# Attention and gated MLP on one core: the low-word step of the float64 weight conversion moved from VectorE to GpSimd

## The chip, the core and the metric

One core of a Trainium2 chip. The metric is the device time of one execution in microseconds; the kernel before takes 406.13 us (median of 3 runs, 405.83 to 406.23). The engines are TensorE (PE in the profile; its weight loads are PEld), VectorE (DVE), ScalarE (ACT), GpSimd (POOL) and SyncE (SP), whose queue issues all transfers of this kernel.

## What is computed

For each of 8 batches and 8 heads, 32 packed queries `p` attend over 576 keys and values, and the 576 queries `q` then attend over the 32 packed results. The heads are put side by side (512 features) and go through a gated layer. Cut to what matters:

```python
p_packed = sm_attn(p, k, v)                  # softmax(p k^T / 8) v
x = sm_attn(q, p_packed, p_packed)           # heads side by side: (8, 576, 512)
h = np.maximum(x @ w_in, 0.0)                # w_in 512 x 1024
conv_out = sum of conv_w[t] * h shifted by t - 1 along the sequence, t = 0, 1, 2
out = (h * sigmoid(conv_out)) @ w_out        # w_out 1024 x 512
```

`q`, `k`, `v` and `p` are float32. `w_in`, `conv_w` and `w_out` are float64, and the kernel has to make float32 of them on the chip.

## The kernel before

The work is cut into 16 groups (a batch and four of its heads), g = 0 to 15. `attention(g)` does both attentions of a group; `packed_weight(b, hf)` multiplies the packed results of a batch into `w_in` (line 609, L609); `ffn1(b, j)` makes one 128-feature block of the hidden layer (matmuls L661; then Relu L673 and scaling L677 on ScalarE, two multiply-adds L679 and L683 on VectorE, Tanh L687 on ScalarE, product L689 on VectorE); `ffn2(m)` multiplies 128 rows by `w_out` (L752, after a split into high and low parts L700 and L703).

The order of all instructions is written out in a table, `ORDER`, of 1525 stream numbers. Each stream is a generator that yields a `Step` (engine, cost in ns, events and buffers it needs) just before it issues its instructions. `Flow.run` takes the streams in the table's order, and every engine executes its own instructions in that order. `Flow` also keeps a planned time for each step, from the costs and from the lags in `LAG` (from engine to engine) and `ISSUE` (for engines whose steps are transfers). That plan has one effect on the program: until the first `ffn2` matmuls, `Flow.fill` puts idle matmuls (`warm`, L244, 216 ns each in the plan) where the plan sees TensorE waiting.

The weights come in eight pieces of 1 MB, i = 0 to 7 (0 to 3 are `w_in`, 4 to 7 `w_out`); L295 issues their transfers in the order 2, 0, 1, 5, 3, 4, 6, 7. They land in three slots, `stage` for i = 2 and 5 and two parts of `spare` (the second `hgt` buffer) for the others; the transfer of piece i waits until piece i - 3 has been converted (`("wp", i - 3)`). `conv_w` has a transfer of its own. Each piece then goes through `narrow`, on 128 partitions with 1024 float64 numbers each, seen as pairs of 32-bit words:

- L265, ScalarE: the upper words, rescaled in place (sets `("up", key)`);
- L267, VectorE: the top three bits of each low word, in place (every second word, so a step of 8 bytes);
- L272, VectorE: upper word shifted left by three, or-ed with those bits, written to `w_in_sb` (i under 4) or to `tmp`.

A piece of `w_out` is then split into `wo_hi` (L323) and `wo_lo` (matmuls L328, copy L332). The L267 step is `loose`: it needs the landed data alone, not the ScalarE step before it in its stream. In the ORDER table it has a place among VectorE's other steps. In the attention, L559, L583 and L417 are transposes on VectorE, L495, L563 and L572 reductions (all of one tensor operand), L565, L578 and L589 have two tensor operands, as L272, L679, L683, L689 and L703 have. L589 makes the low part `a2lo` of the second attention's weights, which L661 needs beside the high part; L629 is the ScalarE copy that makes `glo`, the low part of the folded weight.

Of the kernel before, what the change touches and what calls it, by code (L numbers as in the profile page):

```python
# [63 lines left out]
class Flow:  # L64
# [12 lines left out]
        "PE": dict(PE=0, ACT=197, DVE=196, SP=200, POOL=200),  # L77
        "ACT": dict(PE=216, ACT=153, DVE=142, SP=200, POOL=200),
        "DVE": dict(PE=256, ACT=128, DVE=127, SP=200, POOL=200),
        "DATA": dict(PE=300, ACT=300, DVE=300, SP=0, POOL=0),  # L80
    }
    ISSUE = dict(SP=(465, 1100), POOL=(1050, 1000))
    LATER, LANES = 620, 8
    SLOW = ((4600, 1.28), (5500, 1.7))

# [57 lines left out]
    def transfers(self, step, at):  # L143
        issue, delay = self.ISSUE[step.engine]
        for _ in range(step.parts):
            if step.engine == "SP":
                at = max(at, self.flights.pop(0))
            at += self.LATER if step.engine == "SP" and self.issued >= self.LANES else issue
            self.issued += step.engine == "SP"
            slow = next((x for t, x in self.SLOW if self.data < t), 1.0)  # L150
            self.data = max(self.data, at + delay) + step.ns / step.parts * slow
            if step.engine == "SP":
                self.flights.append(self.data)
        return at, self.data

    def run(self, order):
        for n in order:
# [6 lines left out]
            if engine == "PE":  # L164
# [4 lines left out]
                self.tiled = step.tiled  # L169
            elif step.engine in self.ISSUE:  # L170
                self.free[engine], t = self.transfers(step, at)
# [13 lines left out]
def tile_packed_attention_conv_gate(  # L185
# [11 lines left out]
    nc = tc.nc  # L197
# [61 lines left out]
    def narrow(key, out, raw, m, after=(), take=(), sets=None):  # L259

        pair = raw.rearrange("r (c t) -> r c t", t=2)
        up = pair[:, :, 1]
        low = pair[:, :, 0]
        yield Step("ACT", 93 + m * 14 // 15, after=after, sets=[("up", key)])
        nc.scalar.activation(out=up, in_=up, func=AF.Prelu, scale=F64_REBIAS, alpha=-(2.0**32))  # L265
        yield Step("DVE", 68 + m * 100 // 192, after=after, loose=True)
        nc.vector.tensor_scalar(  # L267
            out=low.bitcast(I32), in0=low.bitcast(U32), scalar1=2.0**-29, scalar2=7.0, op0=ALU.mult, op1=ALU.min
        )
        yield Step("DVE", 69 + m * 100 // 96, after=[("up", key)], take=take, sets=sets)  # L270
        out = out()
        nc.vector.scalar_tensor_tensor(  # L272
            out=out,
            in0=up.bitcast(I32),
            scalar=3,
            in1=low.bitcast(I32),
            op0=ALU.logical_shift_left,
            op1=ALU.bitwise_or,
        )
# [17 lines left out]
    def weight(i):  # L297
# [3 lines left out]
        if i < 4:  # L301
            dst = w_in_sb[:, c : c + 2, cols]
            if src.dtype != F32:
                yield from narrow(i, lambda: dst.bitcast(I32), st, DFF, after, sets=[("wp", i), ("w", i)])
            else:
                yield Step("DVE", 1135, after=after, sets=[("wp", i), ("w", i)])
                nc.vector.tensor_copy(out=dst, in_=st.rearrange("r (c f) -> r c f", c=2))
            return
# [7 lines left out]
        if src.dtype != F32:  # L316
            yield from narrow(i, whole, st, DFF, after, ["x"], [("wp", i)])
        else:
            yield Step("DVE", 1135, after=after, take=["x"], sets=[("wp", i)])
            whole()  # L320
            nc.vector.tensor_copy(out=wide[0], in_=st)
# [12 lines left out]
    def conv_weight():  # L334
        src = conv_w.rearrange("k (j c) -> (k j) c", c=128)
        yield Step("SP", 60, take=["s2"], sets=["cd"])
        st = wk.tile([128, S], F32, name="s2", tag="s2")
        if conv_w.dtype != F32:
            nc.sync.dma_start(out=st[: 3 * NJ, :256].bitcast(I32), in_=src.bitcast(I32))
            yield from narrow("conv", lambda: cw_raw.bitcast(I32), st[: 3 * NJ, :256], 128, ["cd"])  # L340
        else:
            nc.sync.dma_start(out=cw_raw, in_=src)
        yield Step("PE", 20, take=["sm"], give=["s2"], cols=20)
        t = small()
        nc.tensor.transpose(out=t[:, : 3 * NJ], in_=cw_raw, identity=ident[: 3 * NJ, : 3 * NJ])
        yield Step("ACT", 71, give=["sm"], sets=["cw"])
        nc.scalar.copy(out=cw, in_=t[:, : 3 * NJ])
# [473 lines left out]
```

## Time and profile before

| | before |
|---|---|
| median of 3 runs | 406.13 us (405.83 to 406.23) |
| profiled execution: first to last instruction (span) | 404.4 us |
| TensorE busy | 395.5 us, 98% |
| VectorE busy | 340.2 us, 84% |
| ScalarE busy | 275.2 us, 68% |
| GpSimd busy | 0.9 us, 12 instructions |
| chain that ended last | PE 74%, DMA 8%, ACT 8%, DVE 5%, SP queue 3% |
| granted TensorE clock | 1.000 of full speed |

The runs' times include what lies before the first and after the last instruction; the profile has the span alone, so the profiled execution's own time stands only as those 404.4 us, 1.7 us under the median of the runs. Busy time is the union of the instructions of an engine. Matmuls are pipelined, so that a busy TensorE may be running or holding a matmul back; what it waits for is read from the list of waits and from the chain that ended last, which goes back from the last instruction to whatever released each step.

### The profile page before, as it was taken

What the parts mean: (1) busy time and instruction counts of PE and PEld (TensorE: products, weight loads), DVE (VectorE), ACT (ScalarE), POOL (GpSimd) and SP (SyncE); (2) the same over time, 40 slices, a digit from 0 to 9 for tenths busy, and PEclk for the clock granted to TensorE, in tenths of its full rate; (3) what the DMA queues carried; (4) which work ended last, traced back from release to release, by engine and by line L of the source; (5) the groups of instructions that cost most, each with busy time, mean ns of one, the idle gap of its engine ahead of it and who ended that gap; (6) DMA issues with size and microseconds to landing.
All of it is one profiled execution on the core that took longest, in us unless ns stands there. A gap on an engine that the chain in (4) does not pass through costs nothing.

```text
span 404.4 us, 8231 instructions
## 1 busy us (share of the span) xinstructions
PE 395.5 (98%) x3319; PEld 317.6 (79%) x3319; DVE 340.2 (84%) x494; ACT 275.2 (68%) x475; POOL 0.9 (0%) x12
## 2 busy tenths in 40 slices
PE   7899999999999999999999999999999999999996
PEld 6668677787868878888778788788687878887886
DVE  0789999999999999999999999999889886557220
ACT  4889999977668486867566756687666676655121
POOL 0000000000000000000000000000000000000000
PEclk9999999999999999999999999999999999999999
DMA  8999999997947876496563715316001000010211
GB/s 298 366 366 233 293 257 163 137 157 128 134 96 105 129 190 128 88 186 103 107 99 99 151 55 101 129 30 113 28 2 52 28 18 35 26 53 0 78 53 52
DMA packets 140377, 49.19 MB, mean 122 GB/s; under 512 B 121244, under 2 KB 132788, under 8 KB 140340
## 3 DMA queue, kind: packets, MB, share of 16 engines
q1 hardware_dynamic: 140340, 48.67, 53.9%
q8 instruction: 26, 0.43, 0.5%
q14 instruction: 11, 0.09, 0.1%
HBM read 37.25 MB, written 9.44 MB: 115 GB/s over the span
## 4 chain that ended last, share of the span: by engine, by line
PE 74%; DMA 8%; ACT 8%; DVE 5%; SPq 3%; issue 1%; ACTq 0%
PE fo L752 42%; PE big L661 19%; PE sm L752 3%; DMA hgt<-in_moe_w_in_dram 3%; PE big L450 3%; PE big L609 2%; PE sm L535 2%; SPq L515 2%; DMA s<-in_moe_conv_w_dram 2%; DMA v<-in_v_dram 2%; ACT hgt L677 1%; ACT hbuf L673 1%; ACT hgt L687 1%; ACT wo_hi L323 1%; PE big L525 1%
## 5 line engine op out<-in xcount | busy, mean ns | idle before, releaser
L752 PE MATMUL fo<-wo_hi,xhi 128*128 128x512 f32 (+1 forms) x272 | 109.8, 404 | 0.7 <-ACT o L760 0.7
L752 PE MATMUL fo<-wo_hi,xlo 128*128 128x512 f32 (+1 forms) x272 | 106.5, 392 | 0.0
L752 PE MATMUL fo<-wo_lo,xhi 128*128 128x512 f32 (+1 forms) x272 | 106.1, 390 | 0.0
L673 ACT ACTIVATE hbuf<-big 128x576 f32<-128x576 f32 x64 | 41.8, 657 | 32.2 <-PE big L661 32.1
L752 PEld LDWEIGHTS fo<-wo_hi,xhi 128*128 128x128 f32 x272 | 51.2, 188 | 15.7 <-issue 3.0
L679 DVE SCALAR_TENSOR_TENSOR hgt<-hbuf,cw,hgt 128x576 f32<-128x576 f32 x64 | 51.2, 806 | 13.7 <-ACT hgt L677 13.3
L752 PEld LDWEIGHTS fo<-wo_hi,xlo 128*128 128x128 f32 x272 | 51.1, 188 | 12.3
L703 DVE TENSOR_TENSOR xlo<-hgt,xhi 128x1024 fp32r<-128x1024 f32 (+1 forms) x44 | 44.7, 1021 | 16.7 <-ACT xhi L700 16.6
L752 PEld LDWEIGHTS fo<-wo_lo,xhi 128*128 128x128 f32 x272 | 51.1, 188 | 8.5
L661 PE MATMUL big<-a2hi,ghi 128*128 128x288 f32 x256 | 55.8, 299 | 0.1
L687 ACT ACTIVATE hgt<-hgt 128x576 f32<-128x576 f32 x64 | 43.7, 690 | 15.9 <-DVE hgt L683 15.7
L661 PE MATMUL big<-a2hi,glo 128*128 128x288 f32 x256 | 54.4, 294 | 0.0
L661 PE MATMUL big<-a2lo,ghi 128*128 128x288 f32 x256 | 54.2, 293 | 0.0
L683 DVE SCALAR_TENSOR_TENSOR hgt<-hbuf,cw,hgt 128x576 f32<-128x576 f32 x64 | 50.8, 804 | 0.4
L689 DVE SCALAR_TENSOR_TENSOR hgt<-hgt,hbuf 128x576 f32<-128x576 f32 x64 | 47.2, 744 | 4.6 <-ACT hgt L687 4.3
L677 ACT ACTIVATE hgt<-hbuf,cw 128x576 f32<-128x576 f32 x64 | 49.8, 783 | 0.9
L661 PEld LDWEIGHTS big<-a2hi,ghi 128*128 128x128 f32 x256 | 42.9, 188 | 5.9 <-ACT glo L629 1.0
L700 ACT CAST xhi<-hgt 128x1024 fp32r<-128x1024 f32 (+1 forms) x44 | 38.9, 891 | 10.8 <-PE fo L752 6.4
L760 ACT COPY o<-fo 128x512 f32<-128x512 f32 (+1 forms) x34 | 19.6, 578 | 33.3 <-PE fo L752 28.7
L661 PEld LDWEIGHTS big<-a2lo,ghi 128*128 128x128 f32 x256 | 40.9, 188 | 0.0
L661 PEld LDWEIGHTS big<-a2hi,glo 128*128 128x128 f32 x256 | 40.8, 188 | 0.0
L495 DVE TENSOR_REDUCE nm<-big 128x1 f32<-128x576 f32 x16 | 11.9, 746 | 10.6 <-PE big L450 10.6
(91 smaller groups left out, 494.1 us busy)
## 6 DMA issues: line engine op xcount, KB each, us to landing
out_dram<-o SPq DMA_DIRECT2D x35, 256.0 KB, 2.5
v<-in_v_dram SPq DMA_DIRECT2D x16, 512.0 KB, 5.8
k<-in_k_dram SPq DMA_DIRECT2D x48, 144.0 KB, 4.1
q<-in_q_dram SPq DMA_DIRECT2D x48, 144.0 KB, 4.1
hgt<-in_moe_w_in_dram SPq DMA_DIRECT2D x3, 1024.0 KB, 11.2
hgt<-in_moe_w_out_dram SPq DMA_DIRECT2D x3, 1024.0 KB, 6.5
a1T<-stage SPq DMA_DIRECT2D x96, 20.0 KB, 1.8
hgt<-in_k_dram SPq DMA_DIRECT2D x2, 576.0 KB, 5.0
```

Of the source, the lines that this page charges most:

```text
L450: nc.tensor.matmul(out=o.rearrange("c (j r) -> c j r", r=NR) if by_block(g) else o, lhsT=lhs[r, 32 * i : 32 * i + 32], rhs=rhs[r, :, h, :] ...
L661: nc.tensor.matmul(out=t[:, hf, :SH], lhsT=w[:, gg, js], rhs=x[:, hf * SH : (hf + 1) * SH], start=n == 0, stop=n == 3 * NG - 1,)
L673: nc.scalar.activation(out=h[:, 1 : S + 1].rearrange("c (f s) -> c f s", f=2), in_=t[:, :, :SH], func=AF.Relu, scale=0.5)
L677: nc.scalar.activation(out=d, in_=h[:, 1 : S + 1], func=AF.Copy, scale=cw[:, NJ + j : NJ + j + 1])
L679: nc.vector.scalar_tensor_tensor(out=d, in0=h[:, 0:S], scalar=cw[:, j : j + 1], in1=d, op0=ALU.mult, op1=ALU.add)
L683: nc.vector.scalar_tensor_tensor(out=d, in0=h[:, 2 : S + 2], scalar=cw[:, 2 * NJ + j : 2 * NJ + j + 1], in1=d, op0=ALU.mult, op1=ALU.add)
L687: nc.scalar.activation(out=d, in_=d, func=AF.Tanh)
L689: nc.vector.scalar_tensor_tensor(out=d, in0=d, scalar=1.0, in1=h[:, 1 : S + 1], op0=ALU.add, op1=ALU.mult)
L700: nc.scalar.copy(out=hi[:, js, o], in_=src[:, js])
L703: nc.vector.tensor_tensor(out=lo[:, js, o], in0=src[:, js], in1=hi[:, js, o].bitcast(F32), op=ALU.subtract)
L752: nc.tensor.matmul(out=t[:, : fs.stop - fs.start], lhsT=x[:, c, :], rhs=w[:, c, fs], start=c + i == 0, stop=c == NJ - 1 and i == 2)
L760: nc.scalar.copy(out=o[:, fs], in_=sums_of[m, q][:, : fs.stop - fs.start])
```

## The change

L267 is issued on GpSimd instead of VectorE: `nc.gpsimd.tensor_scalar` with the same operands, for the eight weight pieces and for `conv_w`. Its `Step` names POOL, with a planned cost of 120 + 1.5 ns per element. The plan gets a row of lags for POOL, and `ISSUE` loses its POOL entry, since a POOL step is now computation and not a transfer (no step used POOL before). The ORDER table is the same. L272 on VectorE now needs the GpSimd step to be done, as well as the ScalarE step.

```diff
--- before.py
+++ after.py
@@ -77,9 +77,10 @@
         "PE": dict(PE=0, ACT=197, DVE=196, SP=200, POOL=200),
         "ACT": dict(PE=216, ACT=153, DVE=142, SP=200, POOL=200),
         "DVE": dict(PE=256, ACT=128, DVE=127, SP=200, POOL=200),
+        "POOL": dict(PE=260, ACT=200, DVE=200, SP=200, POOL=127),
         "DATA": dict(PE=300, ACT=300, DVE=300, SP=0, POOL=0),
     }
-    ISSUE = dict(SP=(465, 1100), POOL=(1050, 1000))
+    ISSUE = dict(SP=(465, 1100))
     LATER, LANES = 620, 8
     SLOW = ((4600, 1.28), (5500, 1.7))
 
@@ -263,8 +264,8 @@
         low = pair[:, :, 0]
         yield Step("ACT", 93 + m * 14 // 15, after=after, sets=[("up", key)])
         nc.scalar.activation(out=up, in_=up, func=AF.Prelu, scale=F64_REBIAS, alpha=-(2.0**32))
-        yield Step("DVE", 68 + m * 100 // 192, after=after, loose=True)
-        nc.vector.tensor_scalar(
+        yield Step("POOL", 120 + m * 3 // 2, after=after, loose=True)
+        nc.gpsimd.tensor_scalar(
             out=low.bitcast(I32), in0=low.bitcast(U32), scalar1=2.0**-29, scalar2=7.0, op0=ALU.mult, op1=ALU.min
         )
         yield Step("DVE", 69 + m * 100 // 96, after=[("up", key)], take=take, sets=sets)
```

## Rows read from the trace of the kernel before

**Rows 1.** Busy time by stretch: length, then busy us (instructions) of each engine, clock, DMA

```profile
23.00:35.00 12.00, 11.37 (x163) 7.77 (x162) 10.74 (x19) 11.72 (x25) 0.00 (x0) 1.00 1.10 328
...
46.00:72.50 26.50, 26.42 (x262) 18.47 (x259) 26.10 (x41) 26.36 (x46) 0.00 (x0) 1.00 1.03 201
72.50:195.00 122.50, 122.50 (x1106) 100.63 (x1107) 121.02 (x180) 89.61 (x164) 0.00 (x0) 1.00 0.77 130
```

**Rows 2.** What TensorE waited for from 34 us to the end: us, times, longest

```profile
PE fo L752 <- ACT o L760: 0.7, 1, 0.7
PE sm L535 <- DMA v<-in_v_dram: 0.3, 1, 0.3
PE sm L535 <- DMA a1T<-stage: 0.3, 1, 0.3
```

**Rows 3.** The chain of waits from 34 to 76 us: start us, us, what

```profile
23.01 12.23 DMA hgt<-in_moe_w_in_dram
...
36.02 1.14 DVE tmp L272
37.16 0.10 SPq L295
...
37.82 8.01 DMA v<-in_v_dram
...
71.53 0.92 ACT glo L629
...
72.50 3.59 PE big L661 x25
```

**Rows 4.** Line 267 by operation and tile: instructions, ns min/median/max, first and last start

```profile
L267 DVE TENSOR_SCALAR hgt<-hgt x6: 686/694/696, 17.3 to 63.8; 128x1024 int32<-128x1024 uint32 x6
```

**Rows 5.** VectorE in order of time, 35 to 73 us

```profile
35.94 1.21 DVE L272 SCALAR_TENSOR_TENSOR tmp<-stage 128x1024 int32<-128x1024 int32 x1
...
43.04 0.69 DVE L267 TENSOR_SCALAR hgt<-hgt 128x1024 int32<-128x1024 uint32 x1
43.65 0.81 DVE L683 SCALAR_TENSOR_TENSOR hgt<-hbuf,cw,hgt 128x576 f32<-128x576 f32 x1
...
49.74 0.70 DVE L267 TENSOR_SCALAR hgt<-hgt 128x1024 int32<-128x1024 uint32 x1
50.66 0.82 DVE L679 SCALAR_TENSOR_TENSOR hgt<-hbuf,cw,hgt 128x576 f32<-128x576 f32 x1 [0.23 <-ACT hgt L677]
...
55.04 1.33 DVE L417 STREAM_TRANSPOSE kT<-k 128x1152 f32<-128x1152 f32 x1
56.30 0.71 DVE L563 TENSOR_REDUCE mx<-s 128x18 f32<-128x576 f32 x1
...
71.68 0.75 DVE L589 TENSOR_TENSOR a2lo<-a2t,a2hi 128x576 fp32r<-128x576 f32 x1
```

**Rows 6.** GpSimd by line: count, busy us, mean ns, idle before

```profile
masks.py:199 POOL TENSOR_SCALAR_AFFINE_SELECT ident<-ident 128x128 f32<-128x128 f32 x1 | 0.3, 292 | 0.0
L237 POOL MEMSET hbuf<- 128x1 f32 x3 | 0.2, 98 | 0.0
...
masks.py:197 POOL MEMSET ident<- 128x128 f32 x1 | 0.2, 204 | 0.3 <-POOLq L806 0.3
```

**Rows 7.** VectorE in order of time, 13 to 19 us: start us, us

```profile
13.43 0.68 DVE L267 TENSOR_SCALAR stage<-stage 128x1024 int32<-128x1024 uint32 x1
...
14.24 1.21 DVE L272 SCALAR_TENSOR_TENSOR w_in_sb<-stage 128x1024 int32<-128x1024 int32 x1
15.78 0.78 DVE L559 STREAM_TRANSPOSE s<-big 128x576 f32<-128x576 f32 x1 [0.33 <-PE big L450]
```

**Rows 8.** Issues of line 295 for the second matrix: ns min/median/max, first and last start

```profile
L295 SPq DMA_DIRECT2D hgt<-in_moe_w_out_dram x3: 533/625/694, 36.7 to 50.3; - x3
```

**Rows 9.** DMA issues by line for the second matrix: count, KB each, us to landing

```profile
hgt<-in_moe_w_out_dram SPq DMA_DIRECT2D x3, 1024.0 KB, 6.5
```

**Rows 10.** The filling matmuls of line 244: ns min/median/max, first and last start

```profile
L244 PE MATMUL idle<-ident x68: 272/275/580, 1.5 to 48.5; 128*128 128x128 f32 x68
```

## The prediction

> **What bounds the kernel now.** I read the busy times by stretch first. From 72.5 us to 195 us TensorE is busy throughout at a granted clock of 1.00, and in the stretch before it 26.42 of 26.50 us [rows 1]. Busy can hide a held matmul, so the next view is what TensorE waited for: from 34 us to the end three single waits, 0.3, 0.3 and 0.7 us [rows 2]. TensorE is therefore the bound from about 34 us on, and whatever is saved elsewhere after that can give back those waits and little more. The third view, the chain that ended last, says what sets TensorE's pace ahead of 72.5 us: a weight transfer that ends at 35.24 us (piece 3), the L272 of piece 5 soon behind it, an issue on SP, the transfer of `v` that lands at 45.83 us, and then ScalarE back to back until `glo` at 72.45 us, after which TensorE takes over [rows 3]. VectorE stands in that chain for 2 us only, but it has hardly a gap: it is busy 26.10 of 26.50 us up to 72.5 and 121.02 of 122.50 after it [rows 1]. The reader should see two full engines side by side: VectorE can lose nothing without handing it on, while a gain on it meets an equally full TensorE.
>
> **What is removed.** Eight L267 of 128 x 1024, some 0.69 us each [rows 4]; VectorE's next instruction starts 0.61 us after one begins (43.04 to 43.65) [rows 5]. That is 8 x 0.61 = 4.9 us of VectorE's queue; the one on `conv_w` is small and I leave it out.
>
> **What a GpSimd step costs.** No row shows this operation on GpSimd. The nearest that reads and writes SBUF is the affine select of 128 elements, 292 ns; a memset takes 204 ns for 128 elements and 98 ns for one [rows 6]. Slopes: (292 - 98)/127 = 1.53 ns and (204 - 98)/127 = 0.83 ns per element. For 1024 elements this gives 0.10 + 1024 x 1.53 = 1.66 us, or 0.95 us if only the write counts. I take 1.66, because the step reads, computes and writes as the select does. Above, two arithmetic passes would double the select's part: 3.2 us. Bounds 0.95 to 3.2.
>
> **What it does to VectorE beside it.** GpSimd is idle in the rows from 23 us on [rows 1], so no row shows the two engines together. Below, VectorE keeps its pace and nothing is added; a gain in pace is excluded, since the rows leave nothing for it to be freed of. Above, its instructions with two tensor operands stand still for the whole GpSimd step. I take the upper end: L267 on one operand runs at 0.61/1024 = 0.60 ns per element [rows 5] and L272 on two of the same size at 1.21 us, 1.18 ns per element [rows 5], so VectorE fetches some 1.7 words per ns in either; both look like a full read path, and no row shows room for a third stream. The Trainium skill, page SBUF — State Buffer, section Who interferes with whom, speaks against this change: a VectorE instruction with two SBUF inputs and a GpSimd one that reads SBUF exclude each other, and the later one waits for the whole of the other. By that rule the sum is the +2.1 us below; without it, 0; no run here shows which.
>
> **The new wait.** L272 now waits for GpSimd too, and behind L272 stands all of VectorE. Early, piece 2: its L267 ran at 13.43 [rows 7]; on GpSimd it stands behind the 128 elements of `conv_w` (0.3 us by the same slope) and runs from about 13.6 to 15.3 us, while its L272 ran at 14.24 and the transpose behind it at 15.78 [rows 7]. 15.3 + 1.2 is 16.5: 0.7 us late, less the 0.6 of piece 0's L267 that is gone, plus up to 1 us if a subtraction stands behind piece 0's step. I charge none of it to the end, because the chain then runs through a transfer that ends at 35.24 us, and TensorE later waits for `v` at 45.83 [rows 3], with idle matmuls before that; this cover could be short by up to 0.8 us if VectorE's lateness delays that transfer's issue. Pieces 0, 1 and 5 land early enough for their L272.
>
> **The sum, from 35.24 us.** Of VectorE's stream, step by step, with 1.66 us per GpSimd step:
> - Piece 3 lands at 35.24 [rows 3] and holds VectorE until 36.90. The L272 of piece 5 started at 35.94 [rows 5]: +0.96. SP's next weight issue is shown after it, then the `q` and `v` issues [rows 3]; they move by the same, and so does the landing of `v`, less TensorE's 0.3 us wait there.
> - Piece 4, at 43.04: L267 goes (-0.61), and the multiply-add behind it [rows 5] stands for 1.66: +1.05.
> - Piece 6, at 49.74 [rows 5]: the same, +1.05.
> - Piece 7: issued at 50.3 [rows 8], landed 6.5 us later [rows 9], at 56.8. VectorE, late by 3 us less a gap, is then at the transpose L417 and the reduction L563, which have one operand each and ran from 55.04 to 57.01 [rows 5]. They cover the step; L267 goes: -0.61.
> - The 0.23 us gap before 50.66 [rows 5] is filled: -0.23.
>
> 0.96 + 1.05 + 1.05 - 0.61 - 0.23 = +2.2 us at the L589 of 71.68, which ended at 72.43 [rows 5], 0.07 us before TensorE's first matmul that needs `a2lo` at 72.50 [rows 3]. So TensorE starts 2.1 us late there and waits for almost nothing after it that could give time back [rows 2]: +2.1 us on the span of 404.4, 406.5. The median of the runs is 1.7 us above that span, which I carry over: **408.2 us**.
>
> **The idle matmuls.** The plan that places them changes. There are 68 records up to 48.5 us [rows 10], two for each call, so 34 calls at 0.216 us in the plan. They lie where TensorE waits anyway; three calls more or fewer where it doesn't are 0.6 us. I take 0. The rest of the diff issues nothing, and no transfer is moved to or past GpSimd's queue, where nothing else is queued after the start; the transfers still wait for L272 as before.
>
> **The rivals.**
> - *Nothing is felt* (0.26). VectorE keeps its pace beside GpSimd or loses little. Then its stream shortens by 0.61 a piece, but TensorE is full [rows 1] and ScalarE holds the chain up to 72.45 [rows 3]. For it: the engines are separate queues. Against it: VectorE's two-operand work at nearly every landing. It decides below a hold x of (x - 0.70) + 2(x - 0.61) - 0.61 - 0.23 = 0, x = 0.92 us; the lower GpSimd price, 0.95, comes to +0.1 even with a full hold. 406.1 us.
> - *Faster* (0.14). VectorE's relief reaches TensorE: without L267 ahead of it, the L272 of piece 5 starts 0.6 us earlier, SP issues `v` earlier, and TensorE starts 0.6 us earlier at 45.88, where its own 0.3 us wait and a few idle matmuls go; at 197 us the other 0.3 us wait goes too [rows 2]. 0.6 + 0.3 = 0.9 us: 405.2 us. It needs a GpSimd step that holds VectorE for clearly less than 0.61 us. Against it: the transfers ahead of `v` run at a DMA share of 1.10 and 1.03 [rows 1], so an earlier issue need not land earlier.
> - *Much slower* (0.10). GpSimd takes 3.2 us a step. Then piece 3 costs 2.5, pieces 4 and 6 2.6 each, piece 7 3.2 - 1.97 - 0.61 = 0.6, less 0.23: +8.1 us, 414.2 us.
> - *The change only shuffles idle matmuls*, with engines unaffected: inside the first rival's 0.8 us.
>
> **The numbers.** The forecast has the remaining 0.50. Its own range runs from 406.95, where no change ends, to a step of 2.4 us: 1.7 + 1.8 + 1.8 + (2.4 - 1.97 - 0.61) - 0.23 = +4.9, some 410.7 with part of that absorbed in TensorE's waits. A measurement of this kernel tells about 0.2%, 0.8 us, from no change. The whole range takes in the first rival and about half of the faster one: 405.2 to 410.7, which leaves out 0.07 and 0.10. Faster by over 0.2%: 0.14; within: 0.26; slower: 0.50 + 0.10 = 0.60.
>
> **What would show it.** Right: GpSimd rows of about 1.7 us for L267; two-operand rows on VectorE (L679, L683, L272) that last or start 1 to 1.7 us later at each landing, while reductions and transposes beside a step keep their 0.7 to 1.4 us; the L589 near 73.9 us; TensorE's waits up by some 2 us before 75 us and its stretch after 75 us as long as before. Wrong: two-operand rows of unchanged length under a GpSimd step, a TensorE that starts its second batch at 72.5 us or earlier, or a loss that arises after 75 us, where the change issues nothing.

## The result, and the profile after

The kernel after takes 410.09 us (median of 4 runs, 409.56 to 410.15) against 406.18 us for the kernel before on the same chip: 1.0081 times as long, with a 95% interval of 1.0056 to 1.0106. The loss is 3.9 us between the medians and 3.4 us between the two profiled spans (407.8 and 404.4 us). The forecast was 408.2, +2.1 us: the sign was right, the range held, the size was little more than half. The sum behind it was wrong in more than one term, as the rows below show. (The profiled execution of the kernel after is the one of 409.56 us.) Lines of the kernel after stand one further down: L267 is now L268, L272 is L273, L589 is L590.

The first rows to read are what GpSimd does, by line (count, busy us and mean ns, idle time before), against six instructions of 694 ns on VectorE in [rows 4]:

```profile
L268 POOL TENSOR_SCALAR hgt<-hgt 128x1024 int32<-128x1024 uint32 x6 | 24.5, 4078 | 11.2 <-DMA hgt<-in_moe_w_out_dram 6.5 <-DVE hgt L690 2.5 <-DMA hgt<-in_moe_w_in_dram 2.0
L268 POOL TENSOR_SCALAR stage<-stage 128x1024 int32<-128x1024 uint32 x2 | 8.3, 4164 | 4.6 <-DVE sm L575 4.5
```

A step takes 3.8 us at least and 4.1 on average. That is over twice the 1.66 us of the forecast and above its upper bound of 3.2. Two of the steps one by one (start us, us):

```profile
24.71 3.81 POOL L268 TENSOR_SCALAR hgt<-hgt 128x1024 int32<-128x1024 uint32 x1 [2.02 <-DMA hgt<-in_moe_w_in_dram]
...
37.62 3.86 POOL L268 TENSOR_SCALAR hgt<-hgt 128x1024 int32<-128x1024 uint32 x1
```

Next, VectorE in order of time (start us, us; in brackets the idle time before and what ended it), for [rows 5] and [rows 7]:

```profile
17.81 1.23 DVE L273 SCALAR_TENSOR_TENSOR w_in_sb<-stage 128x1024 int32<-128x1024 int32 x1 [2.60 <-POOL stage L268]
...
22.73 1.23 DVE L273 SCALAR_TENSOR_TENSOR w_in_sb<-hgt 128x1024 int32<-128x1024 int32 x1 [1.43 <-POOL hgt L268]
...
25.17 1.28 DVE L579 TENSOR_TENSOR s<-s,sm 128x576 f32<-128x576 f32 x1
...
29.97 1.22 DVE L273 SCALAR_TENSOR_TENSOR w_in_sb<-hgt 128x1024 int32<-128x1024 int32 x1
31.93 0.75 DVE L573 TENSOR_REDUCE sm<-s 128x18 f32<-128x576 f32 x1 [0.74 <-ACT s L570]
...
33.72 1.72 DVE L579 TENSOR_TENSOR s<-s,sm 128x576 f32<-128x576 f32 x1
...
38.05 1.32 DVE L590 TENSOR_TENSOR a2lo<-a2t,a2hi 128x576 fp32r<-128x576 f32 x1
...
40.03 1.21 DVE L273 SCALAR_TENSOR_TENSOR tmp<-stage 128x1024 int32<-128x1024 int32 x1
...
41.23 0.73 DVE L566 TENSOR_TENSOR s<-s,mx 128x576 f32<-128x576 f32 x1
41.89 1.21 DVE L273 SCALAR_TENSOR_TENSOR w_in_sb<-hgt 128x1024 int32<-128x1024 int32 x1
...
52.23 1.21 DVE L273 SCALAR_TENSOR_TENSOR tmp<-hgt 128x1024 int32<-128x1024 int32 x1
...
75.62 0.75 DVE L590 TENSOR_TENSOR a2lo<-a2t,a2hi 128x576 fp32r<-128x576 f32 x1
```

Set their starts against those of the kernel before, of which three more are needed (the L272 of pieces 0, 1 and 3):

```profile
18.59 1.23 DVE L272 SCALAR_TENSOR_TENSOR w_in_sb<-hgt 128x1024 int32<-128x1024 int32 x1
...
27.07 1.22 DVE L272 SCALAR_TENSOR_TENSOR w_in_sb<-hgt 128x1024 int32<-128x1024 int32 x1
...
37.80 1.22 DVE L272 SCALAR_TENSOR_TENSOR w_in_sb<-hgt 128x1024 int32<-128x1024 int32 x1
```

The L272 of piece 2 started at 14.24 before [rows 7] and is 3.57 us later; that of piece 0 is 4.14 later. Two waits for GpSimd have thus made VectorE about as late by 22.73 us as it is at the end. It does not simply stay so late: the L272 of piece 1 is only 2.90 later. Then 0.74 us go to a wait for ScalarE (L570, the exponential, ahead of 31.93), and L579 at 33.72 and L590 at 38.05 last 1.0 and 0.6 us longer than before, beside the GpSimd steps of pieces 5 and 3. The L272 of piece 5, at 35.94 before [rows 5], is 4.09 later, and L589 at 71.68 [rows 5] is 3.94 later. The forecast had the loss arise between 36 and 57 us, at pieces 3, 4 and 6; there VectorE's lateness stays between 3.6 and 4.4 us. The L272 of piece 3 does not wait for GpSimd at all: it starts at 41.89, and the step was done at 41.48 (37.62 + 3.86).

The chain that ended last, by engine on the page:

```profile
PE 88%; ACT 4%; POOL 2%; DMA 2%; DVE 1%; SPq 1%; issue 1%; ACTq 0%
```

DMA had 8% of it and has 2%, TensorE had 74%. In order of time (start us, us, what) the chain shows how the two waits reach TensorE:

```profile
4.69 8.47 DMA s<-in_moe_conv_w_dram
...
13.97 3.81 POOL stage L268
...
17.85 4.86 POOL hgt L268
...
22.73 1.23 DVE w_in_sb L273
...
26.46 0.68 DVE nm L496
...
27.22 0.84 ACT a L500 x2
...
28.10 1.22 PE big L526 x5
29.32 1.92 PE big L435 x9
...
76.44 5.04 PE big L662 x36
```

After the transfer of `conv_w` no transfer stands in it any more: the piece that landed at 35.24 us and the `v` of 45.83 us, both in the chain of before [rows 3], now land before anything needs them (`v` at 47.0 us, and TensorE comes to it at 49.73). They were to cover the early waits; they did not. TensorE's second batch starts at 76.44 us against 72.50 [rows 3].

The list of waits from the start to 80 us (who waited for what: us in total, times, longest) has the two of VectorE, and two of TensorE behind it:

```profile
DVE w_in_sb L273 <- POOL stage L268: 2.6, 1, 2.6
...
PE big L435 <- DVE rs L596: 2.2, 1, 2.2
...
PE big L526 <- ACT a L500: 1.7, 1, 1.7
...
DVE w_in_sb L273 <- POOL hgt L268: 1.4, 1, 1.4
```

From 34 us to the end its one wait is now the 0.7 us at L752 of [rows 2]; the two of 0.3 us are gone, and where they stood some of the loss came back: instruction for instruction, TensorE is 4.23 us late at 35 us, 3.9 from 46 to 195 us and 3.40 from 250 us on.

One more row, by stretch (length, then busy us of PE, PEld, DVE, ACT, POOL, then clock and DMA), had no forecast:

```profile
26.50:28.10 1.60, 0.00 (x0) 0.00 (x0) 1.60 (x3) 0.88 (x3) 1.60 (x1) 1.00 1.16 304
28.10:32.00 3.90, 3.90 (x20) 3.90 (x21) 3.12 (x6) 3.51 (x8) 0.42 (x1) 0.56 1.02 381
```

TensorE ran nothing for the 1.6 us of its wait for L500, and the granted clock behind it is 0.56, near the lower of its two levels (1.2 of 2.4 GHz). Before, the same stretch was at 1.00. Whether this is part of the loss is tested below.

### The profile page after: what moved, and what is told of

It is laid out like the page before. It is cut to its first block, busy times and chain, and to the rows that moved or that the text cites. A ratio compares the mean times of both kernels' runs of the same rounds, so it can differ in the third digit from the quotient of the medians.

```text
span 407.8 us, 8240 instructions
## 1 busy us (share of the span) xinstructions
PE 397.3 (97%) x3319; PEld 319.6 (78%) x3319; DVE 338.2 (83%) x485; ACT 275.3 (68%) x475; POOL 34.4 (8%) x21
## 4 chain that ended last, share of the span: by engine, by line
PE 88%; ACT 4%; POOL 2%; DMA 2%; DVE 1%; SPq 1%; issue 1%; ACTq 0%
PE fo L753 46%; PE big L662 25%; PE big L451 3%; PE sm L753 3%; PE big L610 3%; PE sm L536 2%; DMA s<-in_moe_conv_w_dram 2%; PE big L526 1%; POOL hgt L268 1%; PE big L329 1%; PE big L435 1%; POOL stage L268 1%; PE idle L245 1%; ACT hgt L688 0%; PE sm L552 0%
## 5 line engine op out<-in xcount | busy, mean ns | idle before, releaser
L688 ACT ACTIVATE hgt<-hgt 128x576 f32<-128x576 f32 x64 | 43.9, 694 | 15.9 <-DVE hgt L684 15.6
L268 POOL TENSOR_SCALAR hgt<-hgt 128x1024 int32<-128x1024 uint32 x6 | 24.5, 4078 | 11.2 <-DMA hgt<-in_moe_w_out_dram 6.5
```

Source lines behind the costliest of these rows:

```text
L268: nc.gpsimd.tensor_scalar(out=low.bitcast(I32), in0=low.bitcast(U32), scalar1=2.0**-29, scalar2=7.0, op0=ALU.mult, op1=ALU.min)
L688: nc.scalar.activation(out=d, in_=d, func=AF.Tanh)
```

## The experiments

The theory after the result: **the wait**. VectorE executes its instructions in order; it stands at the L272 of pieces 2 and 0 until a GpSimd step of 3.8 us is done, and hands this lateness on to the end. The rivals: **contention**, in which VectorE and GpSimd take each other's time, as the forecast had it; **the late pieces**, as the forecast's sum had it; and **the clock**. Each run was timed beside the kernel before on the same chip, and its ratio and its difference are taken against that. The edit is made to the kernel before, unless the text says otherwise.

### What a step costs by itself

`e6_prices` runs six GpSimd steps of 512 elements before any data is there, in several forms: every second word or packed, integers or floats, one operation or two.

```diff
+    N = 512
+    two = [w_in_sb[:, c, :].rearrange("r (c t) -> r c t", t=2)[:, :, 0] for c in (2, 3)]
+    one = [w_in_sb[:, c, :N] for c in (2, 3)]
...
+    def price(pair, src, dst, **kw):
+        nc.gpsimd.tensor_scalar(out=pair[1].bitcast(dst), in0=pair[0].bitcast(src), **kw)
+
+    both = dict(scalar1=2.0**-29, scalar2=7.0, op0=ALU.mult, op1=ALU.min)
+    price(two, U32, I32, **both)
+    price(one, U32, I32, **both)
+    price(two, U32, I32, scalar1=2.0**-29, scalar2=None, op0=ALU.mult)
+    price(two, F32, F32, **both)
+    price(one, F32, F32, scalar1=2.0**-29, scalar2=None, op0=ALU.mult)
+    price(two, U32, I32, **both)
```

> The kernel before, with six GpSimd tensor_scalar steps on 128 x 512 elements ahead of the data, nothing waiting for them: as in the change (unsigned in, signed out, step of 8 bytes, two operations), the same on packed words, one operation, float in and out with step 8, float packed with one operation, and the first again. Theory: the step's 3.8 us is its own price, so the first and last take 0.2 + 512 x 3.5 ns = 2.0 us. Rival: it is 1.7 us alone and VectorE stretches it, so about 0.9 us here. Time 406 to 407 us in both.

One run, 406.8 us. By form (count, busy us, mean ns):

```profile
L247 POOL TENSOR_SCALAR w_in_sb<-w_in_sb 128x512 int32<-128x512 uint32 x4 | 7.5, 1876 | 0.3
L247 POOL TENSOR_SCALAR w_in_sb<-w_in_sb 128x512 f32<-128x512 f32 x2 | 3.5, 1764 | 0.2
```

In the order of the diff they took 1.97, 1.92, 1.56, 2.03, 1.49 and 2.05 us. Half the elements cost half of 3.8 us, five of the six times with VectorE nearly idle beside it, so 3.8 us is the step's own price and not contention. From 512 to 1024 elements, 3.81 - 1.97 = 1.84 us for 512 more is 3.6 ns an element. The step of 8 bytes costs next to nothing (1.97 against 1.92), the second operation 0.4 us for 512 elements. The forecast read its slope off an affine select of 128 elements [rows 6], 1.53 ns; the real one is 2.3 times that.

### The wait alone, without the step

`e7_memset_wait` leaves every L267 on VectorE. For pieces 2 and 0, GpSimd copies one column of the converted words and then fills the destination four times, so that L272 has a wait of about 4 us that reads next to nothing. `e11_fill_wait` is the same, with the copy and fills of piece 0 put ahead of its L267.

```diff
+        if key in (0, 2):
+            c, cols, _, _ = weight_tile(key)
+            there = w_in_sb[:, c : c + 2, cols]
+            nc.gpsimd.tensor_copy(out=there[:, 0, 0:1].bitcast(I32), in_=low[:, 0:1].bitcast(I32))
+            for _ in range(4):
+                nc.gpsimd.memset(there, 0.0)
         yield Step("DVE", 69 + m * 100 // 96, after=[("up", key)], take=take, sets=sets)
```

> The kernel before (L267 on VectorE), with the L272 of pieces 2 and 0 made to wait for GpSimd as in the change, but for work that reads nothing: after each of the two L267, GpSimd copies one column of the words and then fills the L272's destination four times (4 x 0.95 us = 3.8 us). Nothing is left out. Theory (the new wait): like the kernel with only the early steps on GpSimd, plus the two L267 that are not taken off VectorE: TensorE's first L661 at 37 to 39 us (34.6 before), 407.8 to 409.5 us. Rival (shared path): no tensor is read on GpSimd, so the loss of the early steps is gone but for the 0.1 to 0.5 us of the wait itself: under 407 us.

414.62 us, 1.0197 times (1.0181 to 1.0213): twice the loss that was to be imitated. The reason is in the trace: the fills of piece 2 ran from 15.91 us, those of piece 0 only from 24.07, since its L267 stood behind piece 2's wait on VectorE. The two waits, 4.1 us each, came one behind the other instead of overlapping. It shows the price of a wait in an in-order queue, but it is not the change's wait; hence the mended form.

> The last run with fills, mended: piece 0's column is copied ahead of its L267, not behind it, so that GpSimd's work for piece 0 starts right after piece 2's and VectorE stands for the L272 of piece 2 until about 18.2 us and for that of piece 0 until about 22.5, as in the kernel with the early steps alone, and GpSimd reads one column of each. Nothing is left out. Theory (the wait alone does it): 408 to 409.5 us, as that kernel (+2.0) plus up to 1 us for the L267 that stay on VectorE. Rival (shared path needed): under 407 us.

411.15 us, 1.0109 times (1.0092 to 1.0126). VectorE in order of time:

```profile
19.27 1.23 DVE L284 SCALAR_TENSOR_TENSOR w_in_sb<-stage 128x1024 int32<-128x1024 int32 x1 [4.12 <-POOL w_in_sb L281]
...
23.87 1.23 DVE L284 SCALAR_TENSOR_TENSOR w_in_sb<-hgt 128x1024 int32<-128x1024 int32 x1 [0.26 <-POOL w_in_sb L272]
```

The two L272 start 5.0 and 5.3 us later than before (3.6 and 4.1 in the kernel after), and TensorE is 5.8 us late at 45 us and 5.25 at the end. Waits of 4.1 and 0.3 us (2.6 and 1.4 in the kernel after) make a loss of 4.8 us here with no GpSimd step beside VectorE's later work. It is more than the change's, and more than was expected: the L267 are still on VectorE, and the fills of piece 2 start at 15.3 us, where the change's step starts at 14.0.

### The early pieces and the late ones

In these four, L267 goes to GpSimd for some keys only. The diff is that of the change with a choice; the tuple is the whole difference. The added lines:

```diff
+        if key in ("conv", 0, 2):
+            yield Step("POOL", 120 + m * 3 // 2, after=after, loose=True)
+            e = nc.gpsimd
+        else:
+            yield Step("DVE", 68 + m * 100 // 192, after=after, loose=True)
+            e = nc.vector
+        e.tensor_scalar(
```

`e2_early_two` has the tuple shown, `e1_late_six` (1, 3, 4, 5, 6, 7), `e13_without_3` (1, 4, 5, 6, 7), `e10_pieces_4_7` (4, 7).

> L267 on GpSimd for conv_w and pieces 2 and 0 alone, on VectorE for the other six. Theory (the new wait): the whole loss comes from VectorE standing still ahead of the L272 of pieces 2 and 0, so 409.5 to 410.5 us, TensorE's first hidden-layer batch (L661 of before) near 39 us as in the changed kernel. Rival (shared path): VectorE is slowed beside every GpSimd step; with two of eight steps left the loss is about a quarter to a third of 3.9 us, 407.2 to 407.6 us.

408.41 us, 1.0045 times (1.0027 to 1.0063): half of the loss, +2.0 us, between the two expectations. The L272 of pieces 2 and 0 start 4.0 and 4.5 us late; by piece 5 VectorE is 2.8 late, and TensorE is 3.0 late at 35 us and 2.2 at the end. So of 4.5 us of lateness some 1.7 are absorbed on the way. VectorE in order of time, the L272 of pieces 2, 0 and 5:

```profile
18.24 1.23 DVE L278 SCALAR_TENSOR_TENSOR w_in_sb<-stage 128x1024 int32<-128x1024 int32 x1 [3.66 <-POOL stage L273]
...
23.12 1.23 DVE L278 SCALAR_TENSOR_TENSOR w_in_sb<-hgt 128x1024 int32<-128x1024 int32 x1 [1.39 <-ACT a1T L534]
...
38.75 1.22 DVE L278 SCALAR_TENSOR_TENSOR tmp<-stage 128x1024 int32<-128x1024 int32 x1
```

Together its waits are longer than those of the kernel after (the second, put down to ScalarE, ends with the GpSimd step at 23.09), and its loss is half. The early waits alone therefore explain half of the 3.9 us; the other half needs the later steps on GpSimd as well.

> The complement of the run with the early steps: L267 of pieces 1, 3, 4, 5, 6 and 7 on GpSimd, of conv_w and pieces 2 and 0 on VectorE. Theory (wait early, hold later): 0.61 us a piece taken off VectorE against a hold of 0.5 to 0.6, and waits at the L272 of pieces 1 and 3 of up to 2 us, of which the wait for v takes a part: 406.8 to 408.3 us. Rival (all loss in the early waits): 406.2 us or under.

410.16 us, 1.0097 times (1.0071 to 1.0123): +3.5 us, where 406.8 to 408.3 was expected. Missed. GpSimd in order of time:

```profile
32.38 3.85 POOL L273 TENSOR_SCALAR stage<-stage 128x1024 int32<-128x1024 uint32 x1 [4.33 <-DMA stage<-in_moe_w_out_dram]
36.30 4.85 POOL L273 TENSOR_SCALAR hgt<-hgt 128x1024 int32<-128x1024 uint32 x1
```

VectorE in order of time:

```profile
41.19 1.23 DVE L278 SCALAR_TENSOR_TENSOR w_in_sb<-hgt 128x1024 int32<-128x1024 int32 x1 [2.11 <-POOL hgt L273]
```

And TensorE's longest wait (us in total, times, longest):

```profile
PE big L440 <- ACT glo L635: 2.2, 1, 2.2
```

Piece 3 queues on GpSimd behind piece 5, its step ends at 41.15 us, and VectorE, on time until there, reaches the L272 of piece 3 (37.80 before) and stands. The folded weight needs that piece, `glo` comes late, and TensorE waits.

> The run with the six later pieces, less piece 3, which goes back to VectorE: GpSimd keeps pieces 1, 4, 5, 6 and 7. Theory: the loss of 3.5 us there came mostly from VectorE standing at the L272 of piece 3, queued on GpSimd behind piece 5; without it five steps with their holds stay and 406.6 to 407.8 us is left. Rival (holds by the shared path in every step): five of six parts of the loss stay, 409.3 us or over.

With piece 3 back on VectorE: 407.98 us, 1.0039 times (1.0024 to 1.0054), +1.6 us over its kernel before where `e1_late_six` has +3.5; just above the 406.6 to 407.8 us that were expected. TensorE is 0.3 us late until 46 us, and 1.75 from 63 us, after a wait of 1.3 us at the L272 of piece 6 (52.29 before, 54.52 here).

> L267 of pieces 4 and 7 alone on GpSimd, the two whose L272 comes over 4 us after the data. No L272 waits. Theory: 2 x 0.61 us off VectorE against two holds of about 0.5, and a full TensorE: 405.9 to 406.8 us, no difference. If VectorE's relief reaches TensorE after all (the faster rival): 405.5 us or under.

Where VectorE has nothing to wait for, pieces 4 and 7, twelve runs give 406.97 us against 406.62, 1.0012 times (1.0000 to 1.0024): no gain and no clear loss. VectorE has no gain to pass on here: two multiply-adds that took 0.81 and 0.80 us before are held beside the two steps, which gives back what the two L267 saved.

```profile
42.74 1.51 DVE L685 SCALAR_TENSOR_TENSOR hgt<-hbuf,cw,hgt 128x576 f32<-128x576 f32 x1
...
57.16 1.33 DVE L685 SCALAR_TENSOR_TENSOR hgt<-hbuf,cw,hgt 128x576 f32<-128x576 f32 x1
```

**The parts do not add.** +2.0 us for the early pieces and +3.5 for the late ones make 5.5, and the change costs 3.9. In the kernel after VectorE is 4.09 us late at the L272 of piece 5, and when it comes to piece 3 at 41.89 GpSimd has been done since 41.48: an early wait pays for a later one. Either alone makes half of the 3.9 us or more.

### What GpSimd takes from VectorE beside it

`e5_side_steps` adds ten GpSimd steps behind the L272 of piece 5, on words that are used up; nothing waits for them. `e8_side_memsets` adds forty fills of 1024 elements in the same place, which write and do not read.

```diff
+        if key == 5:
+            for _ in range(10):
+                nc.gpsimd.tensor_scalar(
+                    out=low.bitcast(I32), in0=low.bitcast(U32), scalar1=2.0**-29, scalar2=7.0, op0=ALU.mult, op1=ALU.min
+                )
```

```diff
+        if key == 5:
+            for _ in range(40):
+                nc.gpsimd.memset(raw[:, :1024], 0.0)
```

> The kernel before, with ten more L267 steps on GpSimd on the used-up words of piece 5 right after its L272, for which nothing waits; nothing is left out. They run from 37 to about 76 us beside a full VectorE. Theory (the new wait): 406.0 to 407.0 us. Rival (shared path, as the prediction had it): with VectorE's two-operand work held for a whole step nearly each time, over 420 us; with 0.5 us a step, 410 to 411 us.

412.20 us, 1.0138 times (1.0114 to 1.0162): above the 410 to 411 us of a hold of 0.5 us a step, and far below the 420. GpSimd's ten steps, in one row:

```profile
37.88 41.97 POOL L282 TENSOR_SCALAR stage<-stage 128x1024 int32<-128x1024 uint32 x10 [36.42 <-DVE tmp L272]
```

VectorE around the step that began at 62.88 us (lines stand five further down here; L688 is L683):

```profile
63.19 1.75 DVE L688 SCALAR_TENSOR_TENSOR hgt<-hbuf,cw,hgt 128x576 f32<-128x576 f32 x1
...
64.92 0.74 DVE L570 TENSOR_TENSOR s<-s,mx 128x576 f32<-128x576 f32 x1
65.59 0.74 DVE L500 TENSOR_REDUCE nm<-big 128x1 f32<-128x576 f32 x1
```

The multiply-add at 63.19 takes 1.75 us in place of 0.81 [rows 5]; the subtraction at 64.92, with two operands as well and under the same GpSimd step (which ends near 67 us), takes its usual time. This repeats: in eight of the ten steps one two-operand instruction, begun 0.2 to 0.95 us into the step, is held 0.4 to 0.95 us, and later ones are not. The length of the hold follows from the step. Take a held instruction's end, less its usual length: in every run with these steps that point lies 2.8 to 2.9 us before the step's end (in the kernel after 25.17 + 1.28 - 0.76 = 25.69, and the step ends at 24.71 + 3.81 = 28.52). So two-operand work is shut out for about the first 1.0 us of a step of 3.8 us, and not after that. VectorE goes from 0.6 to 6.7 us late over ten steps, 0.6 us a step, and TensorE is 6.2 us late behind it. Held for whole steps of 3.8 us, as the forecast had it, VectorE's two-operand work would have lost far more than that.

> The kernel before, with forty GpSimd fills of 128 x 1024 on the used-up words of piece 5 in place of the ten side steps: the same 38 to 40 us of GpSimd beside a full VectorE, nothing waiting, but no reads. If what held VectorE in the run with the side steps (0.6 us a step) is the reading, the time is 406.0 to 407.0 us. If it is any GpSimd work, 409 us or more, and VectorE's two-operand rows stretch again.

407.75 us, 1.0025 times (1.0012 to 1.0037): +1.1 us, between the two expectations. No two-operand instruction is held by the fills; two kinds with one operand are, the small scaling of 18 columns (L574 before) and an L267. GpSimd's fills by line:

```profile
L282 POOL MEMSET stage<- 128x1024 f32 x40 | 39.5, 988 | 38.5 <-DVE tmp L272 36.2
```

VectorE in order of time:

```profile
50.33 1.47 DVE L267 TENSOR_SCALAR hgt<-hgt 128x1024 int32<-128x1024 uint32 x1
...
65.30 1.01 DVE L577 TENSOR_SCALAR sm<-sm 128x18 f32<-128x18 f32 x1
65.37 0.94 DVE L682 SCALAR_TENSOR_TENSOR hgt<-hbuf,cw,hgt 128x576 f32<-128x576 f32 x1
```

The scaling took 0.17 us before and lasts here until a fill is over, the multiply-add behind it with it; the L267 took 0.70. In `e5_side_steps` the same two are held near the end of a GpSimd step. So holding two-operand work takes a GpSimd instruction that reads.

The Trainium skill, page SBUF — State Buffer, section Who interferes with whom, says that a VectorE instruction with two SBUF inputs contends with a GpSimd one that reads SBUF and not with one that only writes, and that a loser is blocked until the other's instruction is over. The first half agrees with these two runs; the second does not hold for two-operand work here, which was held 0.4 to 0.95 us of steps of 3.8 to 4.5 us, and the measurement decides. The small scaling and L267 are both a `tensor_scalar`, which the same section names among the forms that can enter a two-port mode and then contend with GpSimd: that agrees with their being held by fills.

### The order, and the clock

`e4_later_slot` is the kernel after with two entries of the ORDER table moved: the L272 of pieces 2 and 0 (streams 3v and 3r) come later, so that GpSimd has time to finish. `e12_order_only` makes the same move in the kernel before.

```diff
-    "0002043m0408043u0304030305060b3l0c06013k050b060c0g0c0c0b060605053q3v3k0e06070e070a3k063v06063k0j060e3v09060j3s0k"
-    "0f0j0o060k0e0f3n0k0i0h3r3r060k0d063k0e0m0d3k3r060d0r0e0e0d060e060e060m060e0m0r3t0m0m3t0s0r400e3w0w0s0e0s0n0z0e0e"
+    "0002043m0408043u0304030305060b3l0c06013k050b060c0g0c0c0b060605053q3v3k0e06070e070a3k063v06063k0j060e09060j3s0k0f"
+    "0j0o060k0e0f3n0k0i0h3r3r060k0d063k0e0m0d3k060d0r0e0e0d060e060e063v0m060e0m3r0r3t0m0m3t0s0r400e3w0w0s0e0s0n0z0e0e"
```

> The changed kernel with two entries of the order table moved: the L272 of piece 2 after the first attention's transpose into a2t, that of piece 0 behind the next group's first transpose, so that VectorE has other work while GpSimd converts. All eight GpSimd steps stay. Theory (the new wait): most of the 3.9 us comes back, what is left being the later pieces' waits (piece 3 is queued behind piece 5 on GpSimd): 406.5 to 408.5 us. Rival (shared path): the same steps beside the same VectorE work, so 409 to 410.5 us.

407.87 us, 1.0031 times (1.0013 to 1.0049): +1.4 us over its kernel before, against +3.9 for the kernel after.

> The kernel before with the two order-table entries of the later-slot run moved, L267 on VectorE: a control for that run, and a try for a kernel faster than before. Theory: TensorE is tied to transfers there, so 405.8 to 406.8 us; all of the later-slot run's +1.4 then belongs to GpSimd. Rival: the moved order costs 1 us or more itself (407.2 us or over).

407.74 us, 1.0031 times (1.0012 to 1.0049). It was expected near the kernel before, and missed: the later places cost 1.4 us by themselves (407.74 - 406.38), for a reason that was not followed up. Beside each other the two say more than either: in this order L267 costs the same on VectorE (407.74 us, +1.4) and on GpSimd (407.87, +1.4), though all eight steps are there with what they hold. What the change costs thus depends on where the L272 of these two pieces stand in VectorE's order, and not on the step alone; some of GpSimd's cost may hide in the 1.4 us of that order. No kernel run here beats the one before.

`e14_warm` is the kernel after with seven more idle matmuls where TensorE ran nothing from 26.50 to 28.10 us.

```diff
+            if g == 2:
+                warm(7)
             t = big().rearrange("r f s -> r (f s)")
```

> The changed kernel with seven idle matmuls put ahead of the third group's first-attention transposes, where TensorE stood idle from 26.4 to 28.1 us and then ran at a granted clock of 0.56 until 32 us. Nothing is left out. Theory: part of the 3.9 us is not VectorE's lateness but that stretch at the low clock (the transposes behind it took 2.1 us for 9 against 1.2 before, in all about 1.5 us); with TensorE kept busy the clock stays at 1.00 and 0.7 to 1.5 us come back: 408.6 to 409.4 us. Rival (VectorE's lateness sets the pace whatever the clock): 409.9 us or over.

410.18 us, 1.0071 times (1.0045 to 1.0096): +3.3 us, where the kernel after has +3.9 (1.0056 to 1.0106). The intervals overlap, so that nothing is shown to come back. The same stretch of the windows view:

```profile
28.10:32.00 3.90, 3.56 (x30) 3.37 (x30) 3.67 (x7) 3.90 (x10) 0.26 (x1) 1.00 1.02 381
```

The granted clock is back at 1.00, TensorE is 3.4 us late at 33 us in place of 4.2, and then a wait of 1.4 us for `glo` makes it 4.8 from 49 us on. VectorE is 3.9 us late at the L272 of piece 3, nearly as in the kernel after, and 4.8 late behind the next instruction, which is held:

```profile
42.86 1.68 DVE L682 SCALAR_TENSOR_TENSOR hgt<-hbuf,cw,hgt 128x576 f32<-128x576 f32 x1
```

TensorE falls back behind it, so this one trace (of an execution of 411.46 us) does not show what the clock alone is worth. The runs of the kernel after speak against a large share: the one with a mean granted clock of 1.000 took 410.06 us, those with 0.995 and 0.996 took 409.56, 410.15 and 410.11. On the way the stretch does cost time. At 28.1 us TensorE is 3.3 us late both in the kernel after and in `e2_early_two`; then the one runs at a granted clock of 0.56 and the other at 1.00, and at the same transpose some way on (32.08 and 30.33 us) they are 4.3 and 2.5 us late.

## Why the prediction was right, and where not

1. **The GpSimd step** ("I take 1.66 ... Bounds 0.95 to 3.2"): mis-sized. 3.81 us, outside the bounds. The slope came from instructions of 128 elements or fewer [rows 6]; the upper bound, which doubled it for two arithmetic passes, was nearer, though not for its reason: the second operation is 0.4 of 1.97 us. For a step of 3.2 us the prediction's own sum gave 414.2 us.
2. **The early wait** ("I charge none of it to the end"): the step that failed. It was worked out at 0.7 to 1.7 us of lateness, and for that size it may well hold: in `e10_pieces_4_7`, which leaves both pieces as they were, VectorE happens to come to the L272 of piece 0 1.8 us late and is 0.4 late at piece 5. With steps of 3.8 us the lateness is 4.1 us, more than that stretch can absorb (in `e2_early_two` 2.0 us are left at the end), and the transfers named as cover fell out of the chain. In a sum of queue times, cover has a size too: it should have been set against the upper bound of the step.
3. **The late sum** (+0.96, +1.05, +1.05, -0.61, -0.23): none of its positive terms is there. VectorE is 4.14 us late before the first of them and 3.94 after the last. The first was to reach `v` through the L272 of piece 5 and an issue on SP; but SP issues `v` at 38.78 us, before that L272 (40.03), so that the issue does not hang on it. That the sum and the measured loss are of one sign and within 1.8 us of each other is in good part luck: too short a step, held for too long.
4. **The hold** ("stand still for the whole GpSimd step"): mis-sized. Two-operand work is held for at most 1.0 us, once per step, near its start: 0.6 us a step in `e5_side_steps`, the small scaling and an L267 included. That is what each removed L267 gives back [rows 5], so that beside VectorE the exchange is even, as in `e10_pieces_4_7`. The first rival put its turning point at 0.92 us; the hold, 0.6 us, is on its side of that; what beat it was the early wait, with holds that kept VectorE from making it up.
5. **TensorE passes VectorE's lateness on from 72.5 us**: right. 3.94 us late at L589, 3.94 at 76.44, and 3.40 at the end after the later 0.3 us wait of [rows 2] was gone. No stretch after 75 us adds anything.
6. **The relief on VectorE reaches nobody** (against the faster rival): right as far as it can be seen. In the kernel after VectorE is 0.5 us less late behind the missing L267 of piece 4 (4.08 to 3.59) and 0.6 behind that of piece 7 (3.95 to 3.35), waits for ScalarE, and is as late as before. `e10_pieces_4_7` does not test it, since the holds took the relief away.
7. **Idle matmuls**: 68 records after as before [rows 10], the last at 52.4 us in place of 48.5. The zero was right.
8. **What would show it**: GpSimd rows of 1.7 us are 3.8; longer two-operand rows came (L578 at 1.28 and 1.72, L589 at 1.32 us), but instructions at 40.03, 41.23 and 52.23 under a GpSimd step kept their length, which the text named as a sign against the hold; reductions kept theirs, as said.

Not settled: how the other half of the loss divides. The kernel after is 4.1 us late both at piece 0 and at piece 5, where `e2_early_two` recovers from 4.5 to 2.8. On the way it is held at 25, 34 and 38 us (0.52 + 0.98 + 0.60 = 2.1 us, against three L267 less, 1.8 us), and waits 0.74 us for ScalarE, in TensorE's slow stretch; `e2_early_two` has neither. No run takes away the holds alone. Not settled either: the 1.4 us of the moved order. Not tried: piece 3 ahead of piece 5 on GpSimd, and an order table made anew for the longer step.

## What to carry to other kernels

Before moving a step to an idle engine, compare its price there with the distance from its start to its first consumer in the order; where the consumer stands in an in-order queue of a full engine, the difference is paid by everything behind it. Time saved on a full engine beside a fuller one gained nothing in any run here, so such a move had only its risks. When a price is extrapolated from rows eight times smaller, run the sum once at the upper bound and ask of each cover whether it is that long.

## What the runs showed of the hardware

- A GpSimd step with two scalars costs 3.81 us for 128 x 1024 elements and 1.9 to 2.05 for 128 x 512, there for integers or floats, packed or every second word; VectorE does the 1024 in 0.69 us [rows 4].
- A GpSimd instruction that reads holds VectorE's two-operand work once, near its start, for at most 1.0 us; during the last 2.8 us of its 3.8 it does not. GpSimd pays too: its steps took up to 5.0 us when they began beside such an instruction (4.85 at 17.85 us in the kernel after). A fill holds no two-operand work, but held the small scaling of 18 columns and an L267 for 0.8 us.
- After TensorE ran nothing for 1.6 us its granted clock was 0.56 over the next 3.9 us, and 1.00 where idle matmuls filled that gap. A gap does not always do it: after the wait of 2.2 us for L596, earlier in the same trace, the clock stayed at 1.00.
